# A linear-attention block gated by an MLP mixer: list scheduler replaced by tables of order and places

## The chip, the core and the metric

The kernel runs on one core of one Trainium2 chip. The metric is the device time of one execution in microseconds (us); the time before is the median of three runs.

## What is computed

One sequence of S = 2048 rows, D = 512 columns, all in float32. Cut to what matters, the reference is

```python
xn = _layernorm(x)
# A: linear attention, H = 32 heads of 16
q, k, v = split(xn @ wqkv)
phi = lambda t: jnp.where(t > 0, t + 1, jnp.exp(t)) + 1e-6
kv = einsum("bhsd,bhse->bhde", phi(k), v); z = phi(k).sum over s
s = (einsum("bhqd,bhde->bhqe", phi(q), kv) / (einsum("bhqd,bhd->bhq", phi(q), z) + 1e-6)) @ wo
# B: mixer with spatial shifts, then an MLP of width F = 1376
h = _gelu(_layernorm(xn) @ w1)
hs = concat(shift(h[quarter c], (+1, -1, +2, -2)[c]) for c in range(4)) @ w2
x1 = xn + hs
m = x1 + _gelu(_layernorm(x1) @ w3) @ w4
out = x + s * _silu(m)
```

## The kernel before

**Products.** A float32 operand is split into a high part (`...h`, rounded by ScalarE, the engine ACT) and a low part (`...l`, the rest, taken on VectorE, the engine DVE). Each product is then three matmuls on TensorE (PE): high by high, low by high, high by low. Most products of large blocks go through Strassen's scheme with seven products of half blocks (`seven`, L940), whose sums are formed on VectorE. A matmul has 128 rows of weights and 256 or 512 columns.

**Stages.** The 2048 rows are 16 tiles of 128 rows, in four blocks of four tiles. First comes `k` (`raw_k`, L721, with the weights `wk_0` to `wk_3` and the transposed input `xt`, split into `u`), for the first tiles while the weights still arrive; then `q`, the features, the gram matrix for attention, w1 and w2 of the mixer (`mix1`, `mix2`), the first layer of the MLP with attention laid between its pieces (`up_pair`, `up_late`, `attends`), the second layer (`down`, `down_late`), and at the end the gate (`gate`, L1572), which puts `x + s * silu(m)` together and stores it. The second normalisation takes the moments of four tiles at a time: ScalarE squares and sums into `mv`, GpSimd (the engine POOL) makes the columns `w`, `rs` (a power, L622) and `nm`, and ScalarE applies them in `y = o * rs + nm`.

**Planning.** No instruction is issued where the program text names it. Each call of `Plan.mm` (recorded at L147), `act` (L169), `tt` (L192), `ts` (L197), `stt` (L202), `load` (L208), `store` (L213, L215), `fetch` (L220) and `gather` (L226) adds an operation (`Op`) with its engine, its modelled duration and the operations that it must follow, found from the tiles that it reads and writes. 5543 operations are recorded: 3219 for TensorE, 850 for VectorE, 793 for ScalarE, 210 for GpSimd, 471 for the DMA queue of SP. Then `Plan.emit` (L286) issues them in an order of its own. It gives each operation a due time (`deadlines`, `backward`), shifts the due times of some by hand with a table `SOONER` of pairs of operation and quarter microseconds (`nudged`), puts 14 loads at the start in a written turn (`in_turn`), and then plays the five engines forward in a model: it picks the engine that can start soonest and on it, among the operations that can start within 0.02 us (TensorE) or 0.25 us, the one that is due first. TensorE may reach 9 us ahead of its front operation. A tile takes a slot of its pool when its first operation is issued (90 of 512 columns in SBUF, tag `p`; 8 banks of PSUM, tags `acc` and `mm`, among others) and the pools add the waits that a reused slot needs.

What comes out is five fixed lists, one for each engine, with semaphore waits between them; at run time an engine works its list strictly in turn.

## Time and profile before

| | |
|---|---|
| three runs | 497.7, 498.19, 498.9 us; median 498.19 |
| the profiled execution | 498.7 us, span 497.0 us, 1.7 us around it |
| granted TensorE clock | 1.00 |
| TensorE busy | 490.4 us of the span, 3244 matmuls |
| VectorE, ScalarE, GpSimd busy | 432.7, 378.5, 129.5 us |
| DMA | 117.44 MB, mean 236 GB/s |

A row of the timeline gives start and duration in us from the span's start, engine, line, operation, output and inputs without buffer numbers, the shape, the number of merged instructions, and in brackets the idle time before it with what ended that. The duration of a matmul reaches to its modelled end and overlaps the next one's, so the pace is read from starts. Matmuls without a split (inputs `wk_s`, `xt`, `zacc`, `xi`) run in two passes and count as two.

### The profile page before, as it was taken

How to read it: one execution, taken by the hardware profiler on the slowest of the kernel's cores; microseconds unless marked ns; L12 is line 12 of the kernel's file. 1: busy time of each engine (PE TensorE's matmuls, PEld its weight loads, DVE VectorE, ACT ScalarE, POOL GpSimd, SP SyncE). 2: the span in 40 equal slices, each digit the busy share in tenths (PEclk: the TensorE clock that was granted, in tenths of full speed). 3: DMA queues.
4: the chain of work that ended last, by engine and by line, in shares of the span. 5: the costliest groups of instructions: out<-in, count | busy, mean ns of one | idle time of the engine just before them, and what ended most of it. 6: DMA issues, size and time to landing. Idle time of an engine off the chain costs nothing.

```text
span 497.0 us, 9878 instructions
## 1 busy us (share of the span) xinstructions
PE 490.4 (99%) x3244; PEld 445.7 (90%) x3244; DVE 432.7 (87%) x850; ACT 378.5 (76%) x854; POOL 129.5 (26%) x214
## 2 busy tenths in 40 slices
PE   8999999999999999999999999999999999999996
PEld 5788888788888999899898999999999999999996
DVE  4998988898999669999999999999799699779863
ACT  5999999858889789999998567766666785657531
POOL 1483505287831212135200021100000000235320
PEclk9999999999999999999999999999999999999999
DMA  7869895999966899989997499795444699499994
GB/s 223 309 185 287 179 305 169 231 296 281 331 177 173 203 314 254 296 219 274 293 319 206 145 213 290 208 317 177 139 148 146 207 304 345 127 198 288 269 258 151
DMA packets 87082, 117.44 MB, mean 236 GB/s; under 512 B 10328, under 2 KB 39160, under 8 KB 87032
## 3 DMA queue, kind: packets, MB, share of 16 engines
q1 hardware_dynamic: 75512, 96.11, 59.4%
q0 software_dynamic: 11520, 20.71, 24.5%
q8 instruction: 25, 0.41, 0.3%
q14 instruction: 25, 0.20, 0.1%
HBM read 72.66 MB, written 39.93 MB: 227 GB/s over the span
## 4 chain that ended last, share of the span: by engine, by line
PE 95%; ACT 1%; POOL 1%; DMA 1%; DVE 1%; issue 0%; SPq 0%; DVEq 0%
PE pb L147 11%; PE pbd L147 9%; PE h L147 9%; PE g L147 9%; PE pbx L147 6%; PE acc L147 6%; PE pe L147 5%; PE ped L147 5%; PE pbs L147 5%; PE pbm L147 5%; PE q L147 3%; PE k L147 3%; PE pex L147 3%; PE pad L147 3%; PE pa L147 2%; PE pem L147 2%
## 5 line engine op out<-in xcount | busy, mean ns | idle before, releaser
L226 POOL DMA_DIRECT2D xo<-x1d x12 | 10.4, 869 | 168.6 <-ACT d_a111h L169 105.6
L226 POOL DMA_DIRECT2D o<-xnd x16 | 14.0, 911 | 34.2 <-DVE o L192 15.2
L226 POOL DMA_DIRECT2D th<-in_x x14 | 12.6, 903 | 37.5 <-PE pb L147 14.9
L169 ACT ACTIVATE th<-xo 128x512 f32<-128x512 f32 (+1 forms) x16 | 9.8, 616 | 14.4 <-DVE xo L202 11.9
L226 POOL DMA_DIRECT2D zacc<-ke x12 | 11.8, 987 | 27.4 <-DVE xf L192 17.5
L192 DVE TENSOR_TENSOR ht<-h,abc 128x512 f32<-128x512 f32 x16 | 11.0, 689 | 6.9 <-PE h L147 5.8
L226 POOL DMA_DIRECT2D xt<-nrow x16 | 14.6, 1394 | 0.1
L197 POOL TENSOR_SCALAR w<-mv 128x4 f32<-128x4 f32 (+2 forms) x10 | 3.7, 366 | 38.8 <-ACT sq L169 38.5
L169 ACT ACTIVATE y<-o,nm,rs 128x512 f32<-128x512 f32 x16 | 12.3, 807 | 0.5 <-POOL nm L197 0.5
L169 ACT ACTIVATE sq<-o,mv 128x512 f32<-128x512 f32 x16 | 11.5, 726 | 0.2
L202 DVE SCALAR_TENSOR_TENSOR pq<-pq,rd 128x512 f32<-128x512 f32 x16 | 11.0, 690 | 0.4
L202 DVE SCALAR_TENSOR_TENSOR th<-th,so 128x512 f32<-128x512 f32 x12 | 8.2, 687 | 3.4 <-ACT th L169 3.3
L1504 DVE TENSOR_REDUCE den<-qz 128x32 f32<-128x512 f32 x16 | 10.8, 680 | 0.2
L169 ACT ACTIVATE p<-pe 128x256 f32<-128x256 f32 x20 | 7.6, 382 | 4.3 <-PE pe L147 4.2
L169 ACT ACTIVATE u<-pb 128x256 f32<-128x256 f32 x20 | 7.6, 382 | 4.2 <-PE pb L147 4.1
L202 DVE SCALAR_TENSOR_TENSOR qz<-pq,zb 128x512 f32<-128x512 f32 x16 | 10.7, 679 | 0.0
L169 ACT ACTIVATE sq<-o 128x512 f32<-128x512 f32 x16 | 10.1, 635 | 0.8 <-DMA o<-xnd 0.8
L169 ACT ACTIVATE ht<-ht 128x512 f32<-128x512 f32 x16 | 9.8, 625 | 1.0 <-DVE ht L192 0.9
L622 POOL TENSOR_TENSOR rs<-w,nhalf 128x4 f32<-128x4 f32 (+2 forms) x10 | 10.2, 1020 | 0.8
L169 ACT ACTIVATE qe<-qi 128x512 f32<-128x512 f32 x11 | 6.7, 622 | 4.1 <-DVE qi L202 4.1
L169 ACT ACTIVATE x<-x,nm,rs 128x512 f32<-128x512 f32 x12 | 9.2, 806 | 0.0
L169 ACT ACTIVATE sq<-x,mv 128x512 f32<-128x512 f32 x12 | 8.5, 713 | 0.0
(2071 smaller groups left out, 2443.5 us busy)
## 6 DMA issues: line engine op xcount, KB each, us to landing
w_s<-in_w SPq DMA_DIRECT2D x28, 256.0 KB, 5.8
x<-in_x SPq DMA_DIRECT2D x16, 256.0 KB, 6.3
xt<-in_xt SPq DMA_DIRECT2D x16, 256.0 KB, 5.6
xnd<-x SPq DMA_DIRECT2D x16, 256.0 KB, 5.4
xt<-nrow POOLq DMA_DIRECT2D x16, 256.0 KB, 7.7
pqd<-qr SPq DMA_DIRECT2D x16, 256.0 KB, 5.2
o<-xnd POOLq DMA_DIRECT2D x16, 256.0 KB, 6.0
x1d<-o SPq DMA_DIRECT2D x16, 256.0 KB, 5.4
```

What stands on the lines that cost most here:

```text
L147: lambda: nc.tensor.matmul(out.get(), lhs.get(), rhs.get(), start=start, stop=stop, skip_group_check=more))
L169: nc.scalar.activation(out.get(), src.get(), func, scale=get(scale), **kw)
L192: self.vec(eng, out, [a, b], lambda: self.e(eng).tensor_tensor(out.get(), a.get(), b.get(), op=op), True)
L197: lambda: self.e(eng).tensor_scalar(out.get(), a.get(), get(s1), get(s2), **kw), False,
L202: lambda: self.nc.vector.scalar_tensor_tensor(out.get(), a.get(), get(s), b.get(), op0=op0, op1=op1),
L226: lambda: self.nc.gpsimd.dma_start(out.get(), get(src), accum_op=ALU.add), mb=mb)
L622: lambda: g.tensor_tensor(out.get(), src.get(), nh.get(), op=ALU.pow))
L1504: pl.add("DVE", .6, .68, [t], [den], lambda: nc.vector.tensor_reduce(den.get(), t.get().rearrange("p (h d) -> p h d", d=DH), axis=AX.X, op ...
```

## The change

`emit` no longer plans. It takes two tables: `ORDER_OF_ALL`, the numbers of all 5543 operations in the order in which they are issued, and `PLACES`, the slot of every tile in order of the tiles' first mention. It checks that both fit, walks the first table, gives each tile that opens its slot from the second, and issues. The due times, `nudged`, `deadlines`, `in_turn`, `backward`, the marks `soon`, `patience` and `early`, and the table `SOONER` are gone. The operations, what each must follow, their number and their forms are the same; line numbers shift (`mm` from L147 to L133, `act` from L169 to L155, `tt` from L192 to L178, `load` from L208 to L194).

```diff
-    def emit(self, first, lead, reserve, window, ahead, table=()):
-        self.deadlines(first)
-        self.nudged(table)
-        ops = self.ops
...
+    def emit(self, order, places):
+
+        ops, number = self.ops, {}
         for op in ops:
...
+            for t in op.tiles:
+                number.setdefault(t, len(number))
+        if sorted(order) != list(range(len(ops))) or len(places) != len(number):
+            raise RuntimeError("the tables do not fit the operations")
+        held, written = {}, set()
+        for n in order:
+            op = ops[n]
             for t in op.tiles:
                 if t.ap is None:
                     tag = t.tag
-                    if tag in slots:
-                        t.slot = slots[tag].pop(0)[1]
-                        tag += str(t.slot)
+                    if tag in self.counts:
+                        tag += str(places[number[t]])
...
-    pl.in_turn(["wk_s0", "xt0_0", "wk_s0", "xt0_0", "wk_s1", "xt0_1", "wk_s2", "xt0_2", "wk_s3", "xt0_3", "x0", "xt0_1",
-                "xt0_2", "xt0_3"])
-    SOONER = (
-        46, 29, 71, 4, 77, -93, 79, -73, 80, 9, 82, -12, 88, -29, 91, -166, 96, 10, 97, 8, 98, -8, 104, 108,
...
+    ORDER_OF_ALL = (
+        0, 15, 4, 20, 12, 11, 3, 32, 1, 13, 16, 2, 14, 17, 6, 23, 26, 44, 18, 19, 96, 33, 53, 45, 29, 46, 97, 35,
```

On TensorE the median operation moves by 3 places and the farthest by 45; on VectorE by 2 and 20, on ScalarE by 2 and 26. The three places that follow are those of which the prediction speaks. Names carry a buffer number behind the last underscore, which differs between the two programs; `wk_s0` is the loaded first quarter of the weights for `k`, `xt0_0` the first quarter of the transposed input of block 0, `u0_0` the split of the latter.

**The head, SP's DMA queue.** The first loads before:

```order
L208 DMA wk_s0_100<-in_wqkv 128x256
L208 DMA xt0_0_106<-in_xt 128x256
L208 DMA wk_s0_100<-in_wqkv 128x256
L208 DMA xt0_0_106<-in_xt 128x256
L208 DMA wk_s1_118<-in_wqkv 128x512
L208 DMA xt0_1_120<-in_xt 128x256
L208 DMA wk_s2_122<-in_wqkv 128x512
L208 DMA xt0_2_124<-in_xt 128x256
```

and now:

```order
L194 DMA wk_s0_100<-in_wqkv 128x256
L194 DMA xt0_0_103<-in_xt 128x256 x2
L194 DMA wk_s0_100<-in_wqkv 128x256
L194 DMA wk_s1_116<-in_wqkv 128x512
L194 DMA xt0_1_119<-in_xt 128x256
L194 DMA xt0_2_121<-in_xt 128x256
L194 DMA wk_s2_125<-in_wqkv 128x512
L194 DMA wk_s3_127<-in_wqkv 128x512
```

The second half of `xt0_0` has moved ahead of the second half of `wk_s0`, and the quarters of the weights and of the input are no longer strictly in turn.

**The head, TensorE.** Its second to twelfth row before; `k0` to `k3` are the first four tiles of `k`:

```order
L147 MATMUL k0_116<-zacc_86,ones_84 128x512
L147 MATMUL k0_116<-wk_s0_100,xt0_0_106 128x256 x2
L147 MATMUL k2_144<-wk_0h_126,u0_0h_139 128x512
L147 MATMUL k2_144<-wk_0l_136,u0_0h_139 128x512
L147 MATMUL k2_144<-wk_0h_126,u0_0l_142 128x512
L147 MATMUL k3_158<-wk_0h_126,u0_0h_139 128x512
L147 MATMUL k3_158<-wk_0l_136,u0_0h_139 128x512
L147 MATMUL k3_158<-wk_0h_126,u0_0l_142 128x512
L147 MATMUL k1_164<-wk_s0_100,xt0_0_106 128x512
L147 MATMUL k0_116<-wk_1h_146,u0_1h_154 128x512
L147 MATMUL k0_116<-wk_1l_156,u0_1h_154 128x512
L147 MATMUL k0_116<-wk_1h_146,u0_1l_162 128x512
```

and now:

```order
L133 MATMUL k0_114<-zacc_86,ones_84 128x512
L133 MATMUL k0_114<-wk_s0_100,xt0_0_103 128x256 x2
L133 MATMUL k2_145<-wk_0h_123,u0_0h_130 128x512
L133 MATMUL k3_149<-wk_0h_123,u0_0h_130 128x512
L133 MATMUL k2_145<-wk_0l_137,u0_0h_130 128x512
L133 MATMUL k3_149<-wk_0l_137,u0_0h_130 128x512
L133 MATMUL k3_149<-wk_0h_123,u0_0l_143 128x512
L133 MATMUL k2_145<-wk_0h_123,u0_0l_143 128x512
L133 MATMUL k1_162<-wk_s0_100,xt0_0_103 128x512
L133 MATMUL k1_162<-wk_1h_141,u0_1h_154 128x512
L133 MATMUL k0_114<-wk_1h_141,u0_1h_154 128x512
L133 MATMUL k1_162<-wk_1l_159,u0_1h_154 128x512
```

The products of `k2` and `k3`, and of `k0` and `k1`, stood one tile after the other and are now in pairs that share their weights or input part.

**ScalarE before the second layer of the MLP** (around 236 to 241 us of the profile). `y8` to `y11` are four normalised tiles, `f0_0h` the high part of the activated hidden block that TensorE needs for its first full product into `acc`. Before:

```order
L169 ACTIVATE y8_3323<-o8_2796,nm2_96,rs2_93 128x4x4x32
L169 ACTIVATE f0_5h_3334<-gf0_5_3326 128x256
L169 ACTIVATE u20_1_3342<-pb0_1_3291 128x256
L169 ACTIVATE y9_3349<-o9_2901,nm2_96,rs2_93 128x4x4x32
L169 ACTIVATE y10_3359<-o10_2893,nm2_96,rs2_93 128x4x4x32
L169 ACTIVATE y11_3372<-o11_2978,nm2_96,rs2_93 128x4x4x32
L169 ACTIVATE f0_5h_3334<-pb0_0_3213 128x256
L169 ACTIVATE gf0_5_3326<-pb0_0_3213 128x256
L169 ACTIVATE f0_0h_3397<-gf0_0_3250 128x512
L169 ACTIVATE p50_1_3405<-pe0_1_3387 128x256
L169 ACTIVATE gf0_0_3250<-gf0_0_3250 128x512
```

and now:

```order
L155 ACTIVATE p10_1_3317<-pb0_1_3267 128x256
L155 ACTIVATE sq214_3323,mv2_91<-o14_3064 128x512
L155 ACTIVATE f0_5h_3336<-gf0_5_3327 128x256
L155 ACTIVATE y10_3343<-o10_2894,nm2_96,rs2_93 128x4x4x32
L155 ACTIVATE u20_1_3354<-pb0_1_3267 128x256
L155 ACTIVATE y11_3358<-o11_2986,nm2_96,rs2_93 128x4x4x32
L155 ACTIVATE y8_3367<-o8_2812,nm2_96,rs2_93 128x4x4x32
L155 ACTIVATE f0_0h_3378<-gf0_0_3297 128x512
L155 ACTIVATE y9_3386<-o9_2903,nm2_96,rs2_93 128x4x4x32
L155 ACTIVATE gf0_0_3297<-gf0_0_3297 128x512
L155 ACTIVATE p50_1_3400<-pe0_1_3369 128x256
```

`f0_0h` has gone ahead of the fourth `y`, of the second `f0_5h` and of the copy of `gf0_5`. On TensorE its first use stands in row 1223 where it stood in row 1216.

**VectorE between attention and the MLP** (around 293 to 298 us). `yt21l` is the low part of a form of `y` that TensorE needs, `so0` the attention output of tile 0, `qz`, `den`, `rd`, `pq` the steps of its division. Before:

```order
L1504 TENSOR_REDUCE den4_4141<-qz4_4130 128x32
L192 TENSOR_TENSOR yt11l_4151<-yt1f1_4066,yt11h_4079 128x512
L1507 RECIPROCAL rd4_4161<-den4_4141 128x32
L202 SCALAR_TENSOR_TENSOR pq4_3886<-pq4_3886,rd4_4161 128x512
L156 STREAM_TRANSPOSE q4z0_4179<-pq4_3886 128x512
L202 SCALAR_TENSOR_TENSOR qz5_4190<-pq5_4009,zb_2127 128x512
L192 TENSOR_TENSOR so0_4058<-u2s0_3973,pes0_3935 128x256
L1504 TENSOR_REDUCE den5_4208<-qz5_4190 128x32
L192 TENSOR_TENSOR so0_4058<-so0_4058,xo0_4087 128x512
L192 TENSOR_TENSOR yt21l_4230<-yt2f1_4075,yt21h_4095 128x512
L202 SCALAR_TENSOR_TENSOR th0_4186<-th0_4186,so0_4058 128x512
```

and now:

```order
L188 SCALAR_TENSOR_TENSOR qz4_4131<-pq4_3848,zb_2165 128x512
L178 TENSOR_TENSOR so0_4059<-u2s0_3966,pes0_3906 128x256
L1322 TENSOR_REDUCE den4_4147<-qz4_4131 128x32
L178 TENSOR_TENSOR yt41l_4157<-yt4f1_4097,yt41h_4120 128x512
L1325 RECIPROCAL rd4_4168<-den4_4147 128x32
L188 SCALAR_TENSOR_TENSOR pq4_3848<-pq4_3848,rd4_4168 128x512
L188 SCALAR_TENSOR_TENSOR qz5_4183<-pq5_3962,zb_2165 128x512
L142 STREAM_TRANSPOSE q4z0_4191<-pq4_3848 128x512
L1322 TENSOR_REDUCE den5_4198<-qz5_4183 128x32
L178 TENSOR_TENSOR yt21l_4209<-yt2f1_4085,yt21h_4108 128x512
L178 TENSOR_TENSOR q2f1_4220<-q2t_4065,q3t_4088 128x256
L178 TENSOR_TENSOR yt31l_4230<-yt3f1_4070,yt31h_4079 128x512
```

`so0<-u2s0` has gone ahead of `den4`, and `so0<-so0,xo0` behind the rows shown; `yt21l` follows `den5` at once. Its first use on TensorE stands in row 1572 where it stood in row 1567.

More of the change, by code (lines that the diff above doesn't have):

```diff
@@ L82 @@
 class Op:
[L83 to L84 removed]
+    __slots__ = "eng", "busy", "lat", "emit", "pre", "post", "tiles", "two", "table", "mb"
 class Plan:
```

203 lines of the change are left out of this document (11 added, 192 removed), and 393 rows, old and new, of tables (ORDER_OF_ALL, PLACES, SOONER).

## The prediction

> **What bounds the kernel now.** I read the profile's page first (busy times, the granted clock, the chain that ended last), then busy times by stretch, then who waited for whom, and then the timeline of each place where TensorE loses time. The page:
>
> ```profile
> PE 490.4 (99%) x3244; PEld 445.7 (90%) x3244; DVE 432.7 (87%) x850; ACT 378.5 (76%) x854; POOL 129.5 (26%) x214
> PEclk9999999999999999999999999999999999999999
> PE 95%; ACT 1%; POOL 1%; DMA 1%; DVE 1%; issue 0%; SPq 0%; DVEq 0%
> ```
>
> TensorE (PE) is busy for 490.4 of 497.0 us at the full clock, and 95% of the chain that ended last is its matmuls. The change removes no matmul, so an order can only take out what TensorE waits. How much that is, the stretches and the waits tell:
>
> ```profile
> 0.00:13.00 13.00, 11.05 (x34) 7.00 (x35) 6.67 (x14) 7.50 (x17) 1.67 (x11) 1.00 0.78 222
> 200.00:300.00 100.00, 99.80 (x684) 91.66 (x683) 96.48 (x190) 85.24 (x209) 20.65 (x25) 1.00 0.87 248
> ```
>
> ```profile
> PE k L147 <- ACT u_0h L169: 0.9, 1, 0.9
> ```
>
> The first number behind the comma is TensorE's busy time: 11.05 of the first 13 us, 99.80 of the 100 us from 200 on. Busy time hides part of a wait, since the ends of matmuls are modelled and a late one shows as longer; so I take waits from the starts. The pace without a wait is seen in a stretch of eight gaps, through which the output changes five times:
>
> ```profile
> 363.00 0.28 PE L147 MATMUL pb<-yt32h,w_s1l 128*128 128x256 f32 x1
> ...
> 363.95 0.28 PE L147 MATMUL pb<-yt42h,w_b 128*128 128x256 f32 x1
> ```
>
> 0.95 / 8 = 0.119 us for 256 columns. A product of 512 columns takes twice that, 0.23 us (7.01 to 7.24 in the first rows below).
>
> **The change part by part.** The operations are the same; their order on all five engines and their slots are new. Between the two programs the median TensorE instruction moves by 3 places, 3 × 0.119 = 0.36 us, so the change can be weighed place by place: where TensorE waits now, and whether new waits arise.
>
> *The head.* TensorE's rows, the transfer in the chain that its first wait follows, and the rows of ScalarE (ACT) and VectorE (DVE) that release it:
>
> ```profile
> 1.05 1.65 PE L147 MATMUL warm<-ones 128*128 128x128 f32 x6 [1.05 <-POOL ones L538]
> 2.49 1.92 PE L147 MATMUL k<-zacc,ones 128*128 128x512 f32 x2
> 4.20 1.58 PE L147 MATMUL k<-wk_s,xt 128*128 128x256 f32 x4
> 6.68 0.50 PE L147 MATMUL k<-wk_0h,u_0h 128*128 128x512 f32 x1 [0.90 <-ACT u_0h L169]
> 7.01 0.40 PE L147 MATMUL k<-wk_0l,u_0h 128*128 128x512 f32 x1
> 7.24 0.39 PE L147 MATMUL k<-wk_0h,u_0l 128*128 128x512 f32 x1
> ...
> 8.16 1.02 PE L147 MATMUL k<-wk_s,xt 128*128 128x512 f32 x2
> 8.70 0.73 PE L147 MATMUL k<-wk_1h,u_1h 128*128 128x512 f32 x1
> 9.27 0.40 PE L147 MATMUL k<-wk_1l,u_1h 128*128 128x512 f32 x1
> ```
>
> ```profile
> 2.18 4.00 DMA xt<-in_xt
> ```
>
> ```profile
> 6.21 0.42 ACT L169 ACTIVATE u_0h<-xt 128x256 fp32r<-128x256 f32 x1 [2.42 <-DMA xt<-in_xt]
> 7.71 0.63 ACT L169 ACTIVATE wk_1h<-wk_s 128x512 fp32r<-128x512 f32 x1 [1.08 <-DMA wk_s<-in_wqkv]
> 8.25 0.40 ACT L169 ACTIVATE u_1h<-xt 128x256 fp32r<-128x256 f32 x1
> ```
>
> ```profile
> 4.29 0.29 DVE L197 TENSOR_SCALAR wk_0h<-wk_s 128x256 fp32r<-128x256 f32 x1 [4.29 <-DMA wk_s<-in_wqkv]
> ```
>
> The third transfer (second half of `wk_s0`) is there at 4.29, the fourth (second half of `xt0_0`) only at 2.18 + 4.00 = 6.18; `u_0h` follows, and TensorE idles 0.90 us. The change swaps these two. If the fourth place again lands at 6.18, `wk_0h` is ready at 6.18 + 0.29 = 6.47, where `u_0h` now is at 6.21 + 0.42 = 6.63: a gain of 0.1. If it lands near the third, at 4.3 to 4.9, TensorE goes on without the pause, but comes to `u_1h` (ready at 8.25 + 0.40 = 8.65) sooner: the product after the one at 8.70 starts at 9.27, and could start one product (0.23) after about 8.75. So 0.9 at 6.68 shrinks to some 0.3 there. The new order also pairs the products of `k0` and `k1`, so that the low parts get one product more of time; of the 13.00 − 11.05 = 1.95 us without work in the first stretch, 1.05 lie ahead of the first matmul and 0.90 here, so there is hardly a visible wait for them to remove. Against the gain, the first `k` that ScalarE evacuates is complete some places later. Between 0 and 0.5; I take 0.2.
>
> *The wait at 241 us.* Three engines in the order in which they pass it on:
>
> ```profile
> 233.38 2.89 POOL L192 TENSOR_TENSOR nm<-mv,rs 128x4 f32<-128x4 f32 x1
> ```
>
> ```profile
> 236.63 0.81 ACT L169 ACTIVATE y<-o,nm,rs 128x512 f32<-128x512 f32 x1 [0.54 <-POOL nm L197]
> ...
> 237.92 2.22 ACT L169 ACTIVATE y<-o,nm,rs 128x512 f32<-128x512 f32 x3
> ...
> 240.30 0.37 ACT L169 ACTIVATE gf<-pb 128x256 f32<-128x256 f32 x1
> 240.57 0.63 ACT L169 ACTIVATE f_0h<-gf 128x512 fp32r<-128x512 f32 x1
> ```
>
> ```profile
> 240.70 0.40 PE L147 MATMUL acc<-w_10h,f_10l 96*128 96x512 f32 x1
> 241.25 0.50 PE L147 MATMUL acc<-w_0h,f_0h 128*128 128x512 f32 x1 [0.15 <-ACT f_0h L169]
> 241.58 0.32 PE L147 MATMUL pe<-yb220h,w_s1h 128*128 128x256 f32 x1
> ```
>
> The four-column `nm` on GpSimd (POOL) takes 2.89 us, the four `y` wait for it, and `f_0h` stands behind all four and two more. 241.25 − 240.70 − 0.23 = 0.32 us is lost, and 241.58 − 241.25 − 0.23 = 0.10 more on the start after the wait: 0.42. In the new order one `y` (2.22 / 3 = 0.74), the `f_5h` and the `gf` (each 240.57 − 240.30 = 0.27, being of one size) stand behind `f_0h`: it comes 1.28 us sooner, more than the 0.42 that is missing. On TensorE it is asked for seven places later as well. What is late next is `f_0l` on VectorE, two products behind; I count 0.4.
>
> *The wait at 297 us.* VectorE (DVE), then TensorE:
>
> ```profile
> 295.93 0.68 DVE L192 TENSOR_TENSOR so<-so,xo 128x512 f32<-128x512 f32 x1
> 296.53 0.69 DVE L192 TENSOR_TENSOR yt21l<-yt2f,yt21h 128x512 fp32r<-128x512 f32 x1
> ```
>
> ```profile
> 296.94 0.28 PE L147 MATMUL pb<-yb111h,w_al 128*128 128x256 f32 x1
> 297.27 0.39 PE L147 MATMUL pb<-yt21l,w_s0h 128*128 128x256 f32 x1
> 297.50 0.28 PE L147 MATMUL pb<-yb111h,w_ah 128*128 128x256 f32 x1
> ```
>
> 297.50 − 296.94 − 2 × 0.119 = 0.32 us. The new order puts `so<-so,xo` behind `yt21l`, which starts 296.53 − 295.93 = 0.60 sooner, and asks for it five places later on TensorE. That covers the wait: gain 0.32.
>
> *The wait at 402.8.*
>
> ```profile
> 402.57 0.28 PE L147 MATMUL pb<-yb113l,w_ah 128*128 128x256 f32 x1
> 402.76 0.39 PE L147 MATMUL pbs<-m_t3h,q14s1h 128*128 128x256 f32 x1
> ```
>
> 402.76 − 402.57 − 0.12 = 0.07 us; the operands' transfer is issued a few places sooner now. Gain 0.07.
>
> *New waits.* No row of before shows them. The lower end is none at all; the upper is what the old order had in the 480 us behind the head: three such places, 0.42 + 0.32 + 0.07 = 0.8, and twice that where luck is worse. The shortest way from a PSUM tile's last product to the first product of its next user is 7 TensorE places in both orders, about 0.8 us; neither is looser. I take 0.3, nearer to none, since every operation was placed singly here. That products now change their output oftener (1764 of the neighbouring pairs in place of 735) costs nothing by the row at 363.00: the pace is 0.119 with five changes in eight gaps. The Trainium skill ("TensorE: Matmul & The Clock Gate", section "A second HAM failure mode: psum-queue depth-cycling") speaks against such an order: cycling through PSUM banks let TensorE idle so often that its clock fell back and rose again. By that rule the time would rise with the changes; the clock row of the page, 9 in every slice with 735 changes, does not bear it out.
>
> *The tail* is not shortened. The last matmul, ScalarE's part behind it and VectorE's last:
>
> ```profile
> 492.26 0.28 PE L147 MATMUL pbd<-w_l1h,dl1l 96*128 96x256 f32 x1
> ```
>
> ```profile
> 492.58 0.39 ACT L169 ACTIVATE th<-pbd 128x256 f32<-128x256 f32 x1 [1.29 <-PE pbd L147]
> ```
>
> ```profile
> 493.45 0.42 DVE L192 TENSOR_TENSOR th<-th,xr 128x256 f32<-128x256 f32 x1
> ```
>
> From 492.54 to the end at 497.0 are 4.5 us in one chain, its instructions in the same order after the change; so whatever TensorE gains goes through to the end.
>
> *Sum.* The profiled execution took 498.7 us (span 497.0, and 1.7 around it). 498.7 − 0.2 − 0.4 − 0.32 − 0.07 + 0.3 = 498.01. The median of the three runs, 498.19, lies 0.51 under the profiled one: 497.5.
>
> **The rivals.**
>
> *The search takes out nearly all.* The waits read above are 0.9 + 0.42 + 0.32 + 0.07 = 1.7; with all of it gone and no new ones: 498.19 − 1.7 = 496.5. For it: whatever is gained reaches the end. Against it: `u_1h` at 8.65 catches the head. With the head's 0.2 to 0.5 and no new waits it is 1.0 to 1.3, 496.9 to 497.2, which is faster too.
>
> *The clock starts later* (the other side). The two passes of 512 columns at 2.49 take 1.92, the two at 8.16 take 1.02: TensorE begins at half rate and becomes fast about 5 us in, while the four passes at 4.20 run. Today the second pair of those has its weights at 4.29. In the new order it waits for the fourth transfer. If that lands later than about 5.05, when the first pair ends, TensorE stops before the switch, and may work at half rate after 6.2 for up to the time that it took the first time, 1.05 to 5.2: 4.15 us of half rate cost 2.1 us, 1.2 if the switch comes after 2.4 us. The terms behind the head leave −0.49: 497.7 + 1.2 to 2.1 = 498.9 to 499.8. It decides at 5.05. For it: 6.18 in this trace. Against it: it is one straggling transfer in one execution, and the idle 0.90 us at 5.78, after the switch, didn't cool the clock. The Trainium skill (same page, "Part 1: The HAM clock gate") says that the window of activity, some 3.4 us, runs freely and does not start with the kernel; then the cost would change from run to run, which one trace can't show.
>
> *New queues in the middle* (also slower). GpSimd's small operations, like the 2.89 us `nm`, land among other VectorE work than before. With six places like the one at 241, 0.42 each, the sum is 498.19 − 0.79 − 0.2 + 2.5 = 499.7; from three on there is no gain, and slower by more than a measurement's doubt begins at five.
>
> *All of it is moved, nothing gained.* New waits as many as old ones, 0.8 in place of 0.3: 498.0.
>
> **How the numbers follow.** Under 0.2%, about 1.0 us, a measurement can't tell a change of this kernel from none: faster ends at 497.2, slower begins at 499.2. The forecast, with the fourth rival, is the likeliest, 0.42 for "same": 0.7 us lie within it. Faster has 0.40: with no new wait at all 497.5 becomes 497.2, where faster begins, and the first rival lies beyond.  Slower has 0.18: 0.08 for the clock, 0.10 for new queues. The range runs from 496.2, the first rival with 0.3 for short waits that the stretches don't show, to 499.3, which takes in the clock's nearer price.
>
> **What would show it.** Right: TensorE's idle in 13 to 493 us under 0.5, no gap over 0.1 before `acc<-w_0h,f_0h` and `pb<-yt21l`, the passes at 4.20 followed by `k<-wk_0h,u_0h` at 5.8 to 6.7, and 4.5 us from the last matmul to the end. Wrong: matmuls of 256 columns at 0.24 apart beyond 6 us (the clock), or waits of over 0.3 at places where there are none now; or a head that gives back less than 0, by `k` evacuated later.

## The result, and the profile after

The changed kernel takes 501.16 us (median of 11 runs, 499.14 to 503.35), the one before, in turn with it on the same chip, 498.59 (11 runs, 497.7 to 499.92). The ratio is 1.0052, 95% interval 1.0035 to 1.0069: slower by 2.6 us, outside the forecast range (496.2 to 499.3). The profiled execution is one of the 11: 501.16 us, span 499.2. The changed kernel also scatters more: 4.2 us from its fastest to its slowest run, against 2.2.

The page of the changed kernel:

```profile
PE 491.9 (99%) x3244; PEld 446.0 (89%) x3244; DVE 433.2 (87%) x850; ACT 373.6 (75%) x854; POOL 125.1 (25%) x214
PEclk9999999999999999999999999999999999999999
PE 32%; DVE 2%; DMA 2%; ACT 1%; issue 1%; SPq 0%; DVEq 0%
```

The clock is full in every slice. The shares of the chain add up to 38%: it was followed back some 190 us only, so 32% isn't to be set beside the 95% of before. TensorE's idle time is better read by stretch (busy time is the first number behind the comma):

```profile
0.00:13.00 13.00, 11.69 (x38) 7.61 (x39) 7.17 (x16) 7.54 (x18) 2.37 (x11) 1.00 0.76 235
...
100.00:200.00 100.00, 98.84 (x523) 83.52 (x522) 86.38 (x168) 80.65 (x167) 40.34 (x83) 1.00 0.91 250
200.00:300.00 100.00, 99.93 (x683) 92.09 (x682) 97.10 (x195) 85.17 (x209) 16.90 (x24) 1.00 0.88 246
300.00:400.00 100.00, 99.67 (x841) 99.33 (x841) 90.18 (x184) 66.73 (x182) 3.46 (x4) 1.00 0.70 205
```

The head idles 0.64 us less than before (13.00 − 11.69 = 1.31 against 1.95), and the three stretches behind it show 1.16 + 0.07 + 0.33 = 1.56 us of idle where before showed 0.20. The list of TensorE's waits names the places:

```profile
PE pbx L133 <- ACT p1x L155: 0.7, 1, 0.7
PE pbm L133 <- ACT p1m L155: 0.5, 1, 0.5
PE pbs L133 <- DVE so L178: 0.3, 1, 0.3
```

Idle time is not all of it, as the ends of matmuls are modelled. What counts is when the same matmul starts in both traces. Before, then after, five matmuls that stand at the same place in TensorE's list in both, with the same amount of work ahead of them:

```profile
36.74 0.39 PE L147 MATMUL g<-k2h,x2l 128*128 128x512 f32 x1
...
188.39 0.29 PE L147 MATMUL pbm<-w_b11l,ha111h 128*128 128x256 f32 x1
...
253.42 0.28 PE L147 MATMUL pe<-yb220h,w_s1h 128*128 128x256 f32 x1
...
304.14 0.28 PE L147 MATMUL pb<-yb111h,w_ah 128*128 128x256 f32 x1
...
487.62 0.28 PE L147 MATMUL pbd<-wu_31l,d_s31h 128*128 128x256 f32 x1
```

```profile
36.02 0.40 PE L133 MATMUL g<-k2h,x2l 128*128 128x512 f32 x1
...
189.40 0.28 PE L133 MATMUL pbm<-w_b11l,ha111h 128*128 128x256 f32 x1
...
254.12 0.28 PE L133 MATMUL pe<-yb220h,w_s1h 128*128 128x256 f32 x1
...
304.92 0.28 PE L133 MATMUL pb<-yb111h,w_ah 128*128 128x256 f32 x1
...
489.93 0.28 PE L133 MATMUL pbd<-wu_31l,d_s31h 128*128 128x256 f32 x1
```

The changed kernel is 0.72 us ahead at 36, 1.01 behind at 189, 0.70 at 254, 0.78 at 305 and 2.31 at 490. The lead of the head is lost, with 1 us more, by 189; the stretch from 189 to 254, in which the wait at 241 is gone, gives 0.31 back; from 305 on another 1.5 is lost in pieces, most of them too small for the list of waits.

The largest single loss is at 104 us. TensorE, ScalarE, VectorE, GpSimd and SP's queue of the changed kernel, from the wait back to its root:

```profile
103.14 0.39 PE L133 MATMUL pax<-wk_3h,u_3l 128*128 128x512 f32 x1
104.20 0.50 PE L133 MATMUL pbx<-kq_t20h,xs_1h 128*128 128x512 f32 x1 [0.68 <-ACT p1x L155]
```

```profile
103.46 0.69 ACT L155 ACTIVATE p1x<-pbx,rs 128x512 f32<-128x512 f32 x1 [1.24 <-PE pax L133]
```

```profile
76.23 0.69 DVE L188 SCALAR_TENSOR_TENSOR qr<-qe,qi 128x512 f32<-128x512 f32 x1
...
78.30 0.69 DVE L178 TENSOR_TENSOR x7l<-x,x7h 128x512 fp32r<-128x512 f32 x1
...
98.58 0.42 DVE L178 TENSOR_TENSOR xf<-xt,xt 128x256 f32<-128x256 f32 x1 [0.81 <-DMA xt<-nrow]
...
102.57 0.72 DVE L178 TENSOR_TENSOR wt_00l<-wt,wt_00h 128x512 fp32r<-128x512 f32 x1
```

```profile
87.20 3.63 POOL L212 DMA_DIRECT2D xt<-nrow  x4 [2.32 <-DMA xnd<-x]
```

```profile
77.06 0.34 SPq L194 DMA_DIRECT2D xt<-in_xt  x1
79.02 0.33 SPq L194 DMA_DIRECT2D xt<-in_xt  x1
```

`p1x` writes into slot 82, which the table gives it directly after `wt_00`, and VectorE reads `wt_00` until 102.57 + 0.72 = 103.29. (The row names TensorE as the releaser; with this one tile in another slot, below, `p1x` starts at 102.14.) VectorE is late, for the most part because it waited for a transfer that GpSimd issued at 87.20, after a wait for one of SP's queue. On that queue the loads of `xt` go into slots of `qe5` and `x7`, which VectorE reads until 76.23 + 0.69 = 76.92 and 78.30 + 0.69 = 78.99: the queue issues them at 77.06 and 79.02, as soon as their slots come free, and all that is queued behind them waits too. Both ends of the chain are slots that are reused just as the old tile is read. That the late loads are what makes GpSimd's transfer late is only a reading so far; the experiments come back to it.

### The profile page after: what moved, and what is told of

The parts are those of the page before. It is cut to its first block, busy times and chain, and to the rows that moved or that the text cites. A ratio compares the mean times of both kernels' runs of the same rounds, so it can differ in the third digit from the quotient of the medians.

```text
span 499.2 us, 9849 instructions
## 1 busy us (share of the span) xinstructions
PE 491.9 (99%) x3244; PEld 446.0 (89%) x3244; DVE 433.2 (87%) x850; ACT 373.6 (75%) x854; POOL 125.1 (25%) x214
## 5 line engine op out<-in xcount | busy, mean ns | idle before, releaser
L212 POOL DMA_DIRECT2D th<-in_x x14 | 12.5, 922 | 38.9 <-DVE th L188 22.7
L155 ACT ACTIVATE th<-xo 128x512 f32<-128x512 f32 (+1 forms) x16 | 9.8, 615 | 15.8 <-DVE xo L188 7.4
L212 POOL DMA_DIRECT2D xt<-nrow x16 | 15.7, 1388 | 7.6 <-DMA nrow<-ar 3.2
L178 DVE TENSOR_TENSOR ht<-h,abc 128x512 f32<-128x512 f32 x16 | 11.0, 685 | 3.6 <-PE h L133 3.6
L155 ACT ACTIVATE p<-pe 128x256 f32<-128x256 f32 x20 | 7.6, 381 | 7.2 <-PE pe L133 7.2
L155 ACT ACTIVATE y<-o,nm,rs 128x512 f32<-128x512 f32 x16 | 12.7, 810 | 0.2 <-PE acc L133 0.2
L155 ACT ACTIVATE sq<-o,mv 128x512 f32<-128x512 f32 x16 | 11.5, 720 | 0.2
L155 ACT ACTIVATE sq<-o 128x512 f32<-128x512 f32 x16 | 10.0, 627 | 2.1 <-DMA o<-xnd 2.0
L155 ACT ACTIVATE u<-pb 128x256 f32<-128x256 f32 x20 | 7.7, 383 | 3.4 <-PE pb L133 3.3
L155 ACT ACTIVATE ht<-ht 128x512 f32<-128x512 f32 x16 | 9.7, 623 | 0.2
L155 ACT ACTIVATE x<-x,nm,rs 128x512 f32<-128x512 f32 x12 | 9.5, 805 | 0.0
L155 ACT ACTIVATE pa<-pb 128x256 f32<-128x256 f32 x15 | 5.5, 370 | 4.9 <-PE pb L133 4.6
```

The source lines that it names most:

```text
L155: nc.scalar.activation(out.get(), src.get(), func, scale=get(scale), **kw)
L178: self.vec(eng, out, [a, b], lambda: self.e(eng).tensor_tensor(out.get(), a.get(), b.get(), op=op), True)
L212: lambda: self.nc.gpsimd.dma_start(out.get(), get(src), accum_op=ALU.add), mb=mb)
```

## The experiments

Two theories. **P (places):** the order is good, and the new waits come from the table `PLACES`, which reuses a slot of the pool `p` just as it comes free. Its rival **Q (order):** the new order itself puts instructions behind late ones. Later, within P: **E**, ScalarE and VectorE wait for slots, against **D**, SP's queue does, and its loads come late. Where a difference of some tenths matters I give the mean span of a kernel's runs, since the time outside the span differs between programs (last section). The span of before on these chips is 496.35 to 496.7.

**The places chosen anew, first try.** Order kept; each tile takes the slot that has been free longest, with a transfer taken as done when it is issued. 1344 places differ; the first row of the table:

```diff
-        -1, -1, -1, -1, -1, -1, -1, -1, 0, 1, 0, 2, 4, 7, 1, 11, 12, 3, 15, 17, 5, 21, 25, 8, 27, 32, 6, 10,
+        -1, -1, -1, -1, -1, -1, -1, -1, 0, 1, 0, 2, 6, 7, 1, 8, 13, 3, 15, 18, 4, 21, 25, 10, 32, 34, 5, 11,
```

> The changed kernel with its order of all operations, but its SBUF tiles put in other slots: each takes the free slot that was released longest ago; the PSUM banks stay as in the change's table. Theory P (places: the new table reuses SBUF slots just as they come free, so that engines working strictly in turn stop until the last reader of a slot is done, and evacuations of PSUM come late): the wait before 104.2 us (0.9 us, ScalarE's p1x held by the slot that VectorE had just read) goes, and others with it, 1.0 to 2.5 us less than the changed kernel's 501.2: 498.7 to 500.2. Rival Q (order: the new order itself puts evacuations behind other instructions, slots don't matter): 501.2 within 0.4.

Measured: 512.94 us, ratio 1.0301 (1.027 to 1.0333). Both theories missed. TensorE's longest wait behind its start is 2.2 us, for `kvrh` of ScalarE. A slot that a store still reads is not free at its issue; 72 tiles were opened before their slot was. So the places alone, with one and the same order, can cost 11.8 us over the changed kernel. That is not yet an answer for the changed kernel's own places.

**The head alone.** The order and the places of before, written as tables, with the changed order only where TensorE is in its first 12.5 us; the first row of the order:

```diff
-        0, 15, 4, 5, 11, 20, 3, 12, 1, 16, 2, 13, 32, 6, 14, 17, 23, 18, 26, 44, 19, 29, 96, 45, 53, 46, 97, 33,
+        0, 15, 4, 20, 12, 11, 3, 32, 1, 13, 16, 2, 14, 17, 6, 23, 26, 44, 18, 19, 96, 33, 53, 45, 29, 46, 97, 35,
```

> Before's order and places, with the changed order only for the operations up to TensorE's 12.5 us (loads, splits and first products; every slot as before). In the changed trace TensorE had done the same work 0.9 us sooner at 17.7 us and 0.7 sooner at 80 us. If the head's gain is kept: 0.6 to 0.9 less than before's 498.6, 497.7 to 498.0. If later stages hand it back: 498.3 to 498.7.

Measured: 497.76, ratio 0.999 (0.9982 to 0.9999), mean span 0.52 under before's: within the forecast for a gain that is kept. The head's gain is real and is kept to the end.

**Before's order in the tightest places**, transfers again taken as done at issue:

```diff
-        -1, -1, -1, -1, -1, -1, -1, -1, 0, 1, 0, 2, 4, 7, 1, 11, 12, 3, 15, 17, 5, 21, 25, 8, 27, 32, 6, 10,
+        -1, -1, -1, -1, -1, -1, -1, -1, 0, 1, 89, 87, 85, 82, 88, 78, 77, 86, 74, 72, 84, 68, 64, 81, 62, 57, 83, 79,
```

> Before's order of all operations, with SBUF tiles of the large pool put as tightly as before's trace allows: each takes the free slot released last that had been free for at least 0.03 us when its first operation started in that trace; PSUM banks and small pools as before. In before's trace 58 tiles are opened within 0.1 us of their slot's release, here 219, in the changed kernel 128. Theory P: slower by 1.5 to 4 us, 500.1 to 502.6. Rival Q: 498.6 within 0.4.

Measured: 640.58, ratio 1.2854 (1.2815 to 1.2893). Clock row of its page:

```profile
PEclk9997989798889996989989997977999978999799
```

That is 142 us, far beyond either forecast: too blunt to decide between the theories. What it shows is the price of slots that a transfer still holds (below, the same order in tight places costs 0.9 us when transfers' slots are left alone).

**Two of the predicted gains, done by hand** on top of the head: `f0_0h` (2374) ahead of the fourth `y` on ScalarE, and `yt21l` ahead of `so<-so,xo` on VectorE. The first of the two moves:

```diff
-        2425, 2426, 2055, 2427, 2450, 2053, 2051, 2451, 2452, 2453, 2454, 2379, 2455, 2428, 2429, 2054, 2380, 2430, 2431, 2056, 2432, 2374, 2433, 2434, 2382, 2772, 2435, 2383,
+        2425, 2426, 2374, 2055, 2427, 2450, 2053, 2051, 2451, 2452, 2453, 2454, 2379, 2455, 2428, 2429, 2054, 2380, 2430, 2431, 2056, 2432, 2433, 2434, 2382, 2772, 2435, 2383,
```

> The kernel of the head experiment with two more single moves: f_0h on ScalarE goes ahead of the fourth y (and what follows it), and yt21l on VectorE ahead of so<-so,xo. The prediction's own steps: 0.4 and 0.32 less than the head experiment, so 497.0 to 497.3. If the waits at 241 and 297 us are replaced by others: as the head experiment, 497.7 to 498.0.

Measured: 498.24, ratio 0.9994 (0.9985 to 1.0003), above both forecasts. The mean span is 0.26 under before's, where the head alone had 0.52. TensorE in this kernel:

```profile
239.81 0.39 PE L133 MATMUL acc<-w_0h,f_0h 128*128 128x512 f32 x1
...
240.38 0.39 PE L133 MATMUL pe<-yb220h,w_s1h 128*128 128x256 f32 x1 [0.18 <-ACT p L155]
```

The wait for `f_0h` is gone, and 0.57 us later TensorE waits for `p`, which the displaced `y` and `f0_5h` now hold up. The second move fares alike: the product of `yt21l` comes without a wait at 296.18, but that of `yt31l`, which VectorE now finishes too late, starts at 298.29, 0.35 us behind the one before it in place of 0.12. A wait that is moved by hand is not yet removed: the new table also moved TensorE's products there.

**The places chosen anew, second try.** As the first, but with transfers taken as done when their data land in the profiled execution. Tiles that ScalarE or VectorE open within 0.1 us of the release of their slot: 99 in the changed kernel, 34 before, 5 here.

```diff
-        -1, -1, -1, -1, -1, -1, -1, -1, 0, 1, 0, 2, 4, 7, 1, 11, 12, 3, 15, 17, 5, 21, 25, 8, 27, 32, 6, 10,
+        -1, -1, -1, -1, -1, -1, -1, -1, 0, 1, 0, 2, 6, 7, 1, 8, 13, 3, 15, 18, 4, 21, 25, 10, 32, 34, 5, 11,
```

> As the first experiment, but with the DMAs' real ends: the changed kernel's order and PSUM banks, each SBUF tile in the free slot whose last reader ended longest ago, where a DMA counts as a reader until its data has landed in the changed kernel's trace (the first one counted it as done when it was issued, and 72 tiles were opened before their slot was really free). Of the tiles that ScalarE or VectorE opens, 99 start within 0.1 us of their slot's release in the changed trace; by the same ends here 5. Theory P (places): 498.5 to 500.2. Rival Q (order): 501.2 within 0.4.

Measured: 497.28, ratio 0.9982 (0.9973 to 0.9991): faster than before, with the changed kernel's order to the last instruction. That is P, and by 1.2 us more than P's own range allowed; this is the version that beats both kernels.

**One tile moved**, `p1x` at 104 us out of slot 82:

```diff
-        -1, 78, 62, -1, -1, 2, 82, 1, 83, 3, 59, 36, 35, 44, 29, 83, 41, 36, 82, -1, 83, 10, 63, -1, 28, 76, 73, 8,
+        -1, 78, 62, -1, -1, 2, 35, 1, 83, 3, 59, 36, 35, 44, 29, 83, 41, 36, 82, -1, 83, 10, 63, -1, 28, 76, 73, 8,
```

> The changed kernel with one tile moved: p1x12, which ScalarE writes, goes from slot 82 (read last by VectorE until 103.29 us) to slot 35 (free since 102.14). Theory P: the lag of 0.98 us that TensorE took up at 104 us goes: 500.0 to 500.6. Rival Q, or a wait that ends just as late for another reason: 501.2 within 0.4.

Measured: 500.32, ratio 1.0046 (1.0033 to 1.0058). ScalarE starts `p1x` at 102.14 in place of 103.46, without a wait. TensorE:

```profile
104.57 0.50 PE L133 MATMUL g<-k9l,x9h 128*128 128x512 f32 x1 [0.80 <-DVE k9l L188]
```

TensorE stops two products later, for VectorE. The slot of `p1x` was the last link, not the cause: VectorE was late. That the time lies in P's range is luck: the lag that was to go is still there, and the mean span, 498.20, is that of the changed kernel in its second measurement below (498.22).

**Before's order with the head, in the longest-free places.**

```diff
-        -1, -1, -1, -1, -1, -1, -1, -1, 0, 1, 0, 2, 4, 7, 1, 11, 12, 3, 15, 17, 5, 21, 25, 8, 27, 32, 6, 10,
+        -1, -1, -1, -1, -1, -1, -1, -1, 0, 1, 0, 2, 6, 7, 1, 8, 13, 3, 15, 18, 4, 21, 25, 10, 32, 34, 5, 11,
```

> The head experiment (before's order with the changed head) with SBUF slots chosen as in the run above, by before's trace: the slot whose last reader ended longest ago. Of tiles that ScalarE or VectorE opens, 29 in place of 34 start within 0.1 us of the release, so little is to be won: 497.4 to 497.9 by P, 497.8 by Q. Over 498.5 would mean that such tables are upset by a change of slots as such.

Measured: 498.01, ratio 1.0002 (0.9993 to 1.0011). The mean span is 0.08 under before's, where the same order in before's own places was 0.52 under. Long-free places bring this order nothing, and may cost it a little; before's own were loose enough. So they are no gain by themselves, and the second try's lead over before is the order's.

**Before's order, tight where only engines release the slot** (173 tiles opened by ScalarE or VectorE within 0.1 us), transfers' slots left alone:

```diff
-        13, 16, 18, 22, 23, 28, 9, 34, -1, 29, 51, 30, 54, 31, 56, 0, -1, -1, -1, -1, 47, 55, -1, 1, 69, 75, -1, 3,
+        13, 16, 18, 22, 23, 28, 9, 34, -1, 29, 46, 30, 49, 31, 51, 0, -1, -1, -1, -1, 43, 50, -1, 1, 59, 64, -1, 3,
```

> Before's order, with the slots of tiles that ScalarE and VectorE open chosen tight: the free slot that another engine (no DMA) had released last, at least 0.03 us before the opening instruction's start in before's trace. 173 such tiles start within 0.1 us of the release, where before has 34 and the changed kernel 99. Theory P: about as much slower as the changed kernel or more, 1 to 4 us: 499.4 to 502.4. Rival Q: 498.4 within 0.4.

Measured: 498.94, ratio 1.0023 (1.0013 to 1.0033): 0.9 us, between the two forecasts. More tight tiles than the changed kernel's 99 cost a third of what it loses. So a count of tight slots on the engines doesn't give the price.

**The changed kernel and the second try again, side by side** on one chip, without any edit to either.

> The changed kernel once more, on the same chip as the next run. Both theories: 2 to 3.5 us over before. In its trace the waits that come from places should come back where they were (a lag of about 0.9 each at 104 and 181 us); those at 313, 467 and 471 us were 0.5 smaller in the run with one tile moved and may differ again.

> The changed order with the longest-free SBUF slots once more, beside the changed kernel itself, since its first profile fell in a disturbed execution. Theory P: 3 to 4 us under the changed kernel and 0.4 to 1.0 under before, with no lag taken up at 104 and 181 us in the trace; Rival Q: within 1 us of the changed kernel.

Measured: 499.9, ratio 1.004 (1.0028 to 1.0053), against 497.58, ratio 0.9984 (0.9975 to 0.9993). Mean spans 498.22 and 495.35, before 496.47: the places cost 2.87 us (within about 0.7, as the runs scatter), and without them the new order is worth 1.11. The medians lie 2.3 us apart and the changed kernel's 1.7 over before, both a little less than expected. In this execution of the changed kernel TensorE waits twice near 104 us, 0.7 for `u_3h` and 0.9 for `p1x` of ScalarE, and not at 181, where a wait was expected to come back: the loss is there each time, but where it falls changes. TensorE of the second try at the same five matmuls:

```profile
35.79 0.39 PE L133 MATMUL g<-k2h,x2l 128*128 128x512 f32 x1
...
187.81 0.28 PE L133 MATMUL pbm<-w_b11l,ha111h 128*128 128x256 f32 x1
...
252.20 0.28 PE L133 MATMUL pe<-yb220h,w_s1h 128*128 128x256 f32 x1
...
302.60 0.28 PE L133 MATMUL pb<-yb111h,w_ah 128*128 128x256 f32 x1
...
485.84 0.28 PE L133 MATMUL pbd<-wu_31l,d_s31h 128*128 128x256 f32 x1
```

It is ahead of before by 0.95, 0.58, 1.22, 1.54 and 1.78 us (the new order loses 0.37 between 36 and 189 even so). Its first stretch behind 100 us, like the two after it, is busy throughout:

```profile
100.00:200.00 100.00, 100.00 (x530) 84.94 (x529) 86.08 (x169) 81.16 (x172) 38.99 (x83) 1.00 0.91 248
```

SP's queue issues the loads of `xt` earlier than in the changed kernel (the one at 79.02 there is the second here):

```profile
72.34 0.53 SPq L194 DMA_DIRECT2D xt<-in_xt  x1
77.09 0.38 SPq L194 DMA_DIRECT2D xt<-in_xt  x1
```

GpSimd issues its transfer at 85.99 in place of 87.20, and VectorE, which does not wait for it, starts `wt_00l` 1.57 us sooner (0.56 of it is there before the transfer comes in, at the operation ahead of `xf<-xt,xt`, which starts at 96.79 here and at 97.35 there):

```profile
97.13 0.42 DVE L178 TENSOR_TENSOR xf<-xt,xt 128x256 f32<-128x256 f32 x1
...
101.00 0.69 DVE L178 TENSOR_TENSOR wt_00l<-wt,wt_00h 128x512 fp32r<-128x512 f32 x1
```

The instructions themselves are no slower in the changed kernel's places: taken one by one, their durations add up to 438.6 us on ScalarE and 485.8 on VectorE in the second try's trace, and in the changed kernel's first trace to 0.2 less and 0.1 more. So what the places change is when instructions start.

**E against D, first try.** Changed order; new places once only for the tiles whose slot a transfer fills or empties (435 places), once only for the others (1056):

```diff
-        -1, -1, -1, -1, -1, -1, -1, -1, 0, 1, 0, 2, 4, 7, 1, 11, 12, 3, 15, 17, 5, 21, 25, 8, 27, 32, 6, 10,
+        -1, -1, -1, -1, -1, -1, -1, -1, 0, 1, 0, 2, 7, 8, 1, 11, 12, 3, 15, 17, 4, 21, 25, 9, 27, 32, 6, 10,
```

> The changed kernel with new slots first of all for the tiles that a DMA opens (SP's loads and fetches, GpSimd's gathers): each in the slot longest free; of the tiles that an engine opens, 295 had to move as well, since their slot was taken. Started within 0.1 us of the slot's release: of DMA-opened tiles 23 (63 in the changed kernel, 29 in the next run), of those that ScalarE or VectorE opens 78 (99; 18). Theory D (the cost comes by the DMA queues, which stop on a slot and hold what follows): 497.3 to 498.3, as with all slots new. Theory E (it comes by ScalarE and VectorE stopping on a slot): 499.3 to 500.3.

```diff
-        -1, -1, -1, -1, -1, -1, -1, -1, 0, 1, 0, 2, 4, 7, 1, 11, 12, 3, 15, 17, 5, 21, 25, 8, 27, 32, 6, 10,
+        -1, -1, -1, -1, -1, -1, -1, -1, 0, 1, 0, 2, 4, 7, 1, 10, 13, 3, 15, 17, 5, 21, 25, 8, 32, 34, 6, 11,
```

> The counterpart: new slots first of all for the tiles that an engine opens; the DMA-opened keep theirs but for 40 that had to move. Within 0.1 us of the release start 18 tiles that ScalarE or VectorE opens (99 in the changed kernel) and 29 DMA-opened ones (63). Theory E: 497.3 to 498.3. Theory D: about half of the cost left, 498.5 to 499.5. Both near 497.5 would say that either half is enough.

Measured: 509.34 (1.0246, 1.0226 to 1.0266) and 510.07 (1.0235, 1.0212 to 1.0257), 9 us and more over every forecast. Inconclusive: both kernels got waits of their own, the longest of 2.9 us (`kv` for VectorE's `kvt`) in the first and of 6.3 us (`ped` for VectorE's `p5d`) in the second. Probably the tiles that had to keep their slots squeeze the others; that was not followed up.

**E against D, second try.** The other way round: from the second try's places, relations of the changed table (this tile follows that one in its slot) put back. No relation can be put back alone, since the tiles in its way move too: 833 places differ from the second try's in the first of these runs, 1069 in the second, 1119 with both, and 191 for the single tile. First the 30 on which ScalarE or VectorE waited:

```diff
-        81, 31, 42, 69, 4, 88, 71, 10, 0, 71, 32, 46, 54, 39, 75, 82, 15, 2, 85, 65, 86, 42, 11, 71, 37, -1, 20, 48,
+        81, 31, 42, 69, 4, 88, 71, 10, 0, 71, 32, 46, 54, 39, 75, 82, 15, 2, 85, 65, 86, 42, 11, 71, 66, -1, 26, 48,
```

> The changed order with longest-free slots, but 30 tiles of the change's waits of ScalarE and VectorE (p1x12, x12h, x15h, d1_a111h, hs31h and others) open the slot of the same tile as in the change's table; no other tile takes those slots between. Theory E: 2 to 3 us over the table without them, 499.4 to 500.6. Theory D: 497.4 to 497.9.

then the 45 on which SP's queue waited:

```diff
-        12, 16, 19, 24, 23, 29, 9, 27, -1, 28, 51, 33, 60, 30, 55, 0, -1, -1, -1, -1, 46, 54, -1, 1, 78, 80, -1, 3,
+        12, 16, 19, 24, 23, 29, 9, 27, -1, 28, 51, 33, 60, 30, 55, 0, -1, -1, -1, -1, 46, 54, -1, 1, 77, 79, -1, 3,
```

> The same with the 45 tiles for whose slot SP's queue waited in the change (xt0_2, w1_s0, w3_4_s0, h1_ba21xf and others). Theory E: 497.4 to 497.9. Theory D: 499.4 to 500.6.

both (its first changed row is the same as the last one):

> Both kinds put back. If these 75 reused slots are what the change's places cost, about the changed kernel's time, 499.9 to 501.2, by either theory; if it is the rest of the table, 497.4 to 498.5.

and `p1x` behind `wt_00` alone:

```diff
-        81, 31, 42, 69, 4, 88, 71, 10, 0, 71, 32, 46, 54, 39, 75, 82, 15, 2, 85, 65, 86, 42, 11, 71, 37, -1, 20, 48,
+        81, 31, 42, 69, 4, 88, 71, 10, 0, 71, 32, 46, 54, 39, 75, 82, 15, 2, 85, 65, 86, 42, 11, 71, 37, -1, 20, 26,
```

> One tile alone: p1x12 opens the slot of wt_00 as in the change, all else longest free. Theory E: TensorE takes up 0.7 to 1.0 us of lag at 104 us and keeps it: 498.1 to 498.5. If it takes several late slots in a row to stop TensorE: 497.4 to 497.7.

Measured, on one chip with before's mean span at 496.67:

| put back | median us | ratio (95%) | mean span |
|---|---|---|---|
| `p1x` alone | 497.37 | 0.9981 (0.9971 to 0.9991) | 495.52 |
| 30 of the engines | 497.77 | 0.9989 (0.9978 to 0.9999) | 495.59 |
| 45 of SP's queue | 498.04 | 0.9996 (0.9985 to 1.0006) | 496.36 |
| both | 497.93 | 0.9998 (0.9986 to 1.001) | 496.47 |

By these times neither theory holds: the engines' 30 fall in D's range, SP's 45 nearer to E's than to D's, and both together in the range that puts the cost in the rest of the table. With the engines' 30, ScalarE waits as in the changed kernel, and TensorE doesn't:

```profile
103.00 0.69 ACT L155 ACTIVATE p1x<-pbx,rs 128x512 f32<-128x512 f32 x1 [1.10 <-DVE wt_00l L178]
```

```profile
103.81 0.39 PE L133 MATMUL pax<-wk_3h,u_3l 128*128 128x512 f32 x1
104.04 0.39 PE L133 MATMUL pbx<-kq_t20h,xs_1h 128*128 128x512 f32 x1
```

With SP's 45 the last two loads are late, VectorE waits for the transfer, and TensorE for VectorE:

```profile
76.75 0.34 SPq L194 DMA_DIRECT2D xt<-in_xt  x1
78.81 0.33 SPq L194 DMA_DIRECT2D xt<-in_xt  x1
```

```profile
98.99 0.43 DVE L178 TENSOR_TENSOR xf<-xt,xt 128x256 f32<-128x256 f32 x1 [1.67 <-DMA xt<-nrow]
```

```profile
104.81 0.50 PE L133 MATMUL g<-k9l,x9h 128*128 128x512 f32 x1 [0.60 <-DVE k9l L188]
```

So with the queue's slots the step at 104 us comes back, as in the kernel with one tile moved without any help of `p1x`. That does not clear the slot of `p1x` when VectorE is late: in the run with the engines' 30 TensorE comes to `pbx` at 104.04, in the second try at 103.23. It carries this lag of 0.81 from its first 20 us on, and comes too late to be stopped by `p1x`. With `p1x` alone put back, VectorE is on time, `p1x` starts at 101.94, and TensorE does not wait. With both kinds put back there is no step at 104 either: TensorE is 0.98 late when it gets there, 0.6 of it from a wait for VectorE's `wqt` at 18 us.

In span, SP's relations cost 0.84 us beside `p1x` alone, the engines' 0.07, both together 0.95, each within about 0.6. So of the 2.87 two thirds did not come back with these 75 relations.

**Three loads and `p1x`** (the loads of the last three quarters of `xt3`, put back into their slots), and **the second try's rule once more**, with landings from its own profile:

```diff
-        60, 3, 46, 57, 81, 83, -1, 8, 57, 18, -1, 27, 48, -1, 0, 34, -1, 66, 4, -1, 78, 14, 80, 75, 2, 54, 34, 46,
+        60, 3, 46, 57, 81, 83, -1, 8, 57, 18, -1, 27, 48, -1, 0, 34, -1, 66, 43, -1, 78, 14, 80, 75, 2, 54, 34, 46,
```

> The changed order with longest-free slots, but the loads xt3_1, xt3_2 and xt3_3 open the slots that they have in the change's table (held until 79.0, 76.9 and 73.7 us there), and p1x12 the one of wt_00. If this chain is the cause of the step at 104 us: SP issues the loads at about 72, 77 and 79 us and the stores of x behind them up to 3 us later, VectorE's forms of xt start 1.0 to 1.5 us later, and TensorE takes up 0.8 to 1.2 us at 104 us: 498.1 to 498.6. If it takes the rest of the table too: 497.2 to 497.7.

```diff
-        54, 13, -1, 47, 5, 41, 6, 35, 2, 44, 4, 7, -1, 2, 87, 66, 9, 70, 50, 61, 21, 74, 68, 25, 56, 77, 67, 1,
+        54, 15, -1, 47, 5, 41, 6, 35, 2, 44, 4, 7, -1, 2, 87, 66, 43, 28, 50, 61, 21, 74, 68, 25, 56, 2, 32, 1,
```

> The changed order with longest-free slots chosen anew from the trace of the run with such slots (where the first choice went by the ends in the changed kernel's trace); 24 tiles start within 0.1 us of their slot's release in place of 47. If the first choice left nothing: 497.2 to 497.7, the same; if slots still cost: 0.3 to 0.8 less, 496.7 to 497.1.

Measured: 497.79, ratio 0.9992 (0.998 to 1.0003), and 497.32, ratio 0.9984 (0.9974 to 0.9994); spans 495.66 and 495.73. The second choosing of places gains nothing over the first. The three loads (574 places differ from the second try's) make VectorE only 0.3 us late and no step, though the last two are issued at 76.85 and 78.88, as late as with SP's 45, and GpSimd issues its transfers at 87.47, later than in the changed kernel. So a late issue by itself does not stop VectorE. Nine traces of the changed order tell what goes with the wait. GpSimd's transfer is the first of four (`xt<-nrow`, one after another), VectorE waits for the last of them, and on SP's queue stands a load of `wr`:

| run (times in us) | first of the four issued | longest of them to landing | load of `wr` issued | VectorE waits |
|---|---|---|---|---|
| changed | 87.20 | 9.6 | 89.87 | 0.81 |
| changed again | 88.13 | 10.1 | 90.18 | 1.86 |
| one tile moved | 87.04 | 9.7 | 89.56 | 1.02 |
| 45 of SP's queue | 87.79 | 9.4 | 89.77 | 1.67 |
| second try | 85.99 | 8.8 | 86.98 | none |
| `p1x` alone | 86.82 | 8.4 | 87.05 | none |
| three loads and `p1x` | 87.47 | 8.1 | 87.37 | none |
| 30 of the engines | 87.59 | 8.3 | 87.83 | none |
| both | 87.34 | 8.5 | 90.66 | none |

VectorE waits where the transfers take longest to land. In these four executions the load of `wr` is issued 2.0 to 2.7 us behind the first of them, while all four are on their way; SP's queue had stood 2.7 to 2.9 us before it, until a `pax` product of TensorE was done, and a load of an input has only its slot to wait for. In four of the five without a wait it is issued within 1.0 us of the first. The run with both is the exception: the load is late and the landing quick, in an execution in which TensorE and VectorE are 1.0 to 1.3 us late anyway. So the slot of `wr` is the likely link between SP's queue and the step. No run puts it back alone.

## Why the prediction was wrong

The step that failed is *New waits*: "I take 0.3, nearer to none, since every operation was placed singly here." Its upper end was 1.6, twice the old waits. The new waits measure some 3 us (2.87 in span between the changed kernel and its own order in other places), and 0.25 of the 2.6 is time outside the span. The sign that was named for a wrong forecast came true: waits of 0.7, 0.5 and 0.3 at places that had none. I priced them by the old waits and by PSUM's round trips, and left out the second table: that an operation is placed singly in the order says nothing of whether its slot is free. The diff showed `PLACES`, and the order's text says that an SBUF slot adds a wait when it is reused; which tile follows which in a slot could have been read from the table.

*The head* had the right mechanism and was sized too low: 0.2 counted, 0.52 to 0.72 measured (the head alone; the trace at 36 us). The fourth transfer landed at 4.73, within the 4.3 to 4.9 of the better case, and TensorE went on without a pause, at 5.43 and so even before the 5.8 to 6.7 that was named as a sign. VectorE's and TensorE's rows of the changed kernel:

```profile
4.73 0.29 DVE L183 TENSOR_SCALAR wk_0h<-wk_s 128x256 fp32r<-128x256 f32 x1 [4.73 <-DMA wk_s<-in_wqkv]
```

```profile
5.43 0.81 PE L133 MATMUL k<-wk_0h,u_0h 128*128 128x512 f32 x2
...
8.29 0.73 PE L133 MATMUL k<-wk_1h,u_1h 128*128 128x512 f32 x2 [0.26 <-ACT u_1h L155]
```

The pause before `u_1h` shrank to 0.26, about the 0.3 foreseen.

*The wait at 241* (0.4) went as worked out, 0.12 us from one start to the next:

```profile
241.23 0.28 PE L133 MATMUL pe<-yt10h,w_s0l 128*128 128x256 f32 x1
241.35 0.39 PE L133 MATMUL acc<-w_0h,f_0h 128*128 128x512 f32 x1
```

*The waits at 297 and 402.8* are gone too: in the changed kernel the first products of `yt21l` (298.42) and of `m_t3h` (404.14) stand 0.11 to 0.12 us from their neighbours on both sides. *The tail* was right in size. The last matmul of the changed kernel:

```profile
494.57 0.28 PE L133 MATMUL pbd<-w_l1h,dl1l 96*128 96x256 f32 x1
```

From 494.57 + 0.28 = 494.85 to 499.2 are 4.35 us, where 4.5 was forecast. So the four gains hold, and the order in good places is worth 1.11 us of span where 0.99 had been summed. That the second try's 497.28 to 497.58 is the forecast's 497.5 is luck all the same: the head gave more than counted, the order lost 0.37 elsewhere, and 0.3 more lies outside the span.

*The rivals.* "New queues in the middle" gave 499.7 and the right side, and named queues on GpSimd; the queue that the runs show at 104 us is SP's, and the cause slots. It had 0.10. "The clock starts later" did not happen in the changed kernel: 4.73 lies ahead of the 5.05 from which it decides. What it left open, whether the start of full rate moves from run to run, the other traces answer: it does (last section). "The search removes nearly all" (496.9 to 497.2) is more than the order gives even without its places. The Trainium skill ("TensorE: Matmul & The Clock Gate", section "A second HAM failure mode: psum-queue depth-cycling") would have let the time rise with the changes of the output; the clock row stayed at 9 with 1764 of them, and the same order ran faster than before in other places, so by the trace that rule has no part in the 2.6 us.

*Open.* That the places cost the time is shown: one order in three tables of long-free places (the second try, run twice, its rule once more, and `p1x` alone) is 2.3 to 3.9 us faster than in `PLACES`. How they cost it is shown in part. About 1.9 of the 2.87 us did not come back with the relations that were put back. At 104 us SP's slots bring the step back, by a link that is likely and not tested; the losses at 181 us and from 305 on are placed in time and not traced to slots one by one. That several near misses have to coincide, which would also fit the larger scatter of the runs, was argued and not shown.

## What to carry to other kernels

A table or allocator that says where tiles lie is part of the order: for each tile, compare the time at which its slot is last read (for a store: at which the data have landed) with the time at which its next user wants it, and look at loads first, since a load that waits holds up everything behind it in its queue. Judge an order and its places apart, by running the same order with the slots that have been free longest. Here, within 2% of TensorE's busy time, the table of slots gave back 2.87 us where the order gains 1.11.

## What was not expected of the hardware

- Slots that a store reads are free only when the data have landed. Taking them as free at the issue cost 15.7 us in the changed order (512.94 against 497.28 by the same rule with the landing) and, with the tightest places, 142 us in before's.
- TensorE's full rate does not come at the same time in each execution. In the trace of before, the first passes of 256 columns start 0.43 us apart (4.20, 4.62, 5.05); in that of the same order with 173 tight tiles they start 0.21 apart from 4.09 on, and in that with the three loads put back 0.43 apart until 5.48. In the second of these it gained nothing, as the next product waited for `u_0h` until 6.69, in place of 6.68.
- In the 142 us kernel the granted clock fell in many slices (mean 0.921, lowest digit 6), while TensorE was still busy 84% of the span; the longest of its pauses is 8.8 us, for `xo` of VectorE. In the changed kernel, with pauses of at most 0.7 us behind its start, the clock row stays at 9.
- The time outside the span is nearly a constant of each program, and not of its work: 1.7 us on average in 12 of the programs run (before among them), 1.9 to 2.0 in the changed kernel, the second try and two of their near relatives, and 2.15 and 2.18 in two with relations put back. Of the 2.6 us by which the changed kernel is slower, 0.25 is this. What sets it stays open.
